# The second layer's gate and value products: four of six token groups in pairs by Strassen's seven block products

## The chip, the cores and the metric

The kernel runs on one core of a Trainium2 chip. The metric is the device time of one execution in microseconds; the median of three runs is quoted. In the profile PE is the matrix engine (TensorE) and PEld its weight loads, DVE is VectorE, ACT is ScalarE, POOL is GpSimd, and SP is the engine whose queue issues the DMAs. PE reads operands from SBUF and writes to PSUM, which has eight banks of 512 fp32 columns by 128 partitions. "2.4 GHz" is the clock that the profile shows as a granted clock of 1.00.

## What is computed

Attention with a block-causal mask over 4 x 8 heads of 576 positions and 64 dimensions gives 2304 tokens of 512 features. Two feed-forward layers follow; the change lies in the second.

```python
x = attention(q, k, v)                  # (2304, 512), tokens by features
h = x @ w_in                            # 512 -> 2048
x = (h - tanh(h)) @ w_out               # 2048 -> 512
xn = x / sqrt(mean(x * x) + 1e-6) * rms_g
g = xn @ w_gate                         # 512 -> 1536
val = xn @ w_val                        # 512 -> 1536
out = (silu(g) * val) @ w_out2          # 1536 -> 512
```

The weights arrive as float64 and are turned into fp32 on the chip, from pairs of 32-bit words.

## The kernel before

Tokens are taken in six groups of 384 (`NG`, `TG`), each three tiles of 128 (`TT`). The hidden features of the second layer go in twelve units of 128 (`J2`). To keep fp32 accuracy, every operand of a product is held as a high part (rounded to fp32r) and a low part (the rest); a product is three matmuls, high by high, high by low and low by high. ACT rounds the high part (`rnd`, L98) and DVE subtracts it for the low part (`lo`, L103).

Second layer, from L849: for each group `n` and unit `j`, PE makes the gate product and the value product. Each takes four slices of 128 input features by three matmuls of 384 columns (L862 to L864), twelve in all, into a PSUM bank of the pool `gvp` (four banks). ACT applies SiLU to the gate (L871), DVE multiplies by the value (L872), ACT and DVE split the result into `gh`, `gl`. The output matmuls of the unit before follow (`out2`, `gemm_out` L679 to L681: nine of 512 columns, into one PSUM accumulator for each token tile). After unit 11 the accumulators are copied out (L843, L845) and stored.

The inputs of the next group are prepared in units 3 to 8: `xn_a` loads a tile and scales it (L710), `xn_b` transposes it on PE (four transposes of 128x128, L718) and splits it.

The second layer's weights stay in SBUF, as high and low parts. There are 36 pieces of [128, 512] (`w2_piece`): gate, value and output weights of each unit. Each is loaded (`stage`), made into floats (`convert`: two passes on ACT, L133 and L135, three on DVE, L136 to L138) and split. 18 pieces are made during the first layer's last group, 18 during the second layer's first group.

What sets the order: PE's instructions run as the code is written (`manual_schedule`), those of the other engines in an order that a scheduler fixes when the program is built; each engine executes its queue strictly in order. SP's queue carries all the DMAs named here.

Of the kernel before, what the change touches and what calls it, by code (L numbers as in the profile page):

```python
# [49 lines left out]
EARLY = 7  # L50

# [38 lines left out]
def build(ctx, tc, q, k, v, w_in, w_out, w_gate, w_val, w_out2, rms_g, ident_in, out):  # L90
# [18 lines left out]
    w1f = [drm.tile([128, 1024], F32, name=f"w1f_{j}") for j in range(J1 // 2)]  # L109
    w1d = [[drm.tile([128, 1024], F32, name=f"w1d_{x}_{j}") for j in range(J1)] for x in "io"]  # L110
# [461 lines left out]
    with tc.manual_schedule(engines={PE.engine}):  # L572
# [133 lines left out]
        def xn_a(n, t):  # L706
            c = n * TT + t
            x = w2a.tile([128, DM], F32, name="xin", tag="xin", bufs=2)
# [15 lines left out]
        w2 = {}  # L724

        def w2_piece(n, pool):
            j, part = divmod(n, 3)
            if part == 0:
                w2[j] = [[pool.tile([128, 512], F32R, name=f"w2_{j}_{x}_{y}") for y in "hl"] for x in range(3)]
            st = stage(rows_(w_out2, j) if part == 2 else cols((w_gate, w_val)[part], j))  # L730
            convert(st, *w2[j][part])
# [4 lines left out]
        npc = 0  # L736
        nld = J1
        for s in range(NSA):
# [54 lines left out]
            if j == J1 - 1:  # L793
                while att.pos < goal:
                    att.step()
                if g == NG - 2:
# [4 lines left out]
                    env["stg"] = sw.enter_context(tc.tile_pool(name="st2", bufs=3, side="right"))  # L801
# [4 lines left out]
            if g == NG - 1:  # L806
# [6 lines left out]
                for _ in range(2 if j % 7 == 3 else 1):  # L813
                    w2_piece(npc, w2a)
                    npc += 1
# [9 lines left out]
        gvp = ctx.enter_context(tc.tile_pool(name="gvp", bufs=2, space=PSUM))  # L825
# [3 lines left out]
        def out2(s, t):  # L829
            n, j = divmod(s, J2)  # L830
            if j == 0:
                accs[t] = accp.tile([128, DM], F32, name=f"acc{t}", tag=f"acc{t}")
            gh, gl = gts[s]
            wh, wl = w2[j][2]
            gemm_out(accs[t], gh, gl, wh, wl, t, j == 0, j == J2 - 1)
            if j == J2 - 1:
                c = n * TT + t
                if s == NSB - 1 and t == TT - 1:
                    o = w2a.tile([128, DM], F32, name="xin", tag="xin", bufs=2)
                else:  # L840
                    o = wk.tile([128, DM], F32, name="x2s", tag="x2s")
# [7 lines left out]
        NSB = NG * J2  # L849
        for s in range(NSB):  # L850
            n, j = divmod(s, J2)
            if n == 0 and npc < 3 * J2:
                w2_piece(npc, w2b)
                npc += 1
            xh, xl = xt("B", n)
            gv = []
            for part in range(2):
                ps = gvp.tile([128, TG], F32, name=f"gv{part}", tag=f"gv{part}")
# [7 lines left out]
                if part == 0:  # L866
                    if n == 0 and npc < 3 * J2:
                        w2_piece(npc, w2b)
                        npc += 1
# [17 lines left out]
        for t in range(TT):  # L887
            out2(NSB - 1, t)
# [20 lines left out]
```

## Time and profile before

| | |
|---|---|
| median of three runs | 1095.95 us (1094.66 to 1096.4) |
| span of the profiled execution | 1093.2 us |
| PE busy | 1067.0 us (98%), 5696 matmuls |
| DVE busy | 613.8 us (56%) |
| ACT busy | 542.6 us (50%) |
| POOL busy | 158.5 us (14%), none of it after about 560 us |
| DMA | 172.3 MB |

The profiled execution's own device time is not given apart from its span. Matmuls overlap in the record, so PE's busy share says only that it was rarely empty; what a matmul takes is seen from the starts of neighbours. The second layer's first product starts at 626.6 us, so that layer takes the last 467 us of the span.

### The profile page before, as it was taken

How to read it: one execution, taken by the hardware profiler on the slowest of the kernel's cores; microseconds unless marked ns; L12 is line 12 of the kernel's file. 1: busy time of each engine (PE TensorE's matmuls, PEld its weight loads, DVE VectorE, ACT ScalarE, POOL GpSimd, SP SyncE). 2: the span in 40 equal slices, each digit the busy share in tenths (PEclk: the TensorE clock that was granted, in tenths of full speed). 3: DMA queues.
4: the chain of work that ended last, by engine and by line, in shares of the span. 5: the costliest groups of instructions: out<-in, count | busy, mean ns of one | idle time of the engine just before them, and what ended most of it. 6: DMA issues, size and time to landing. Idle time of an engine off the chain costs nothing.

```text
span 1093.2 us, 16380 instructions
## 1 busy us (share of the span) xinstructions
PE 1067.0 (98%) x5696; PEld 951.3 (87%) x5696; DVE 613.8 (56%) x1403; ACT 542.6 (50%) x1271; POOL 158.5 (14%) x276
## 2 busy tenths in 40 slices
PE   7799989999999999999999999999999999999998
PEld 5576669998889999999999899899999999999997
DVE  5888857777678766676567889622222222222212
ACT  5777757667677665566556687512112111111111
POOL 5531201123323232323300000000000000000000
PEclk8999999999999999999999999999999999999999
DMA  9788888988777979766589855200000000000000
GB/s 217 230 282 296 264 285 261 285 218 232 178 188 201 249 212 240 224 203 192 157 299 395 294 165 183 83 34 21 29 10 20 29 11 20 29 11 1 29 1 30
DMA packets 166962, 172.32 MB, mean 158 GB/s; under 512 B 108000, under 2 KB 131680, under 8 KB 166880
## 3 DMA queue, kind: packets, MB, share of 16 engines
q1 hardware_dynamic: 166880, 171.28, 52.0%
q8 instruction: 45, 0.74, 0.3%
q14 instruction: 37, 0.30, 0.1%
HBM read 140.84 MB, written 30.41 MB: 157 GB/s over the span
## 4 chain that ended last, share of the span: by engine, by line
PE 91%; ACT 3%; DVE 3%; DMA 1%; issue 1%; SPq 0%; POOL 0%; DVEq 0%
PE acc L681 9%; PE acc L679 9%; PE acc L680 9%; PE gv L864 9%; PE gv L862 9%; PE gv L863 9%; PE t L766 6%; PE t L768 6%; PE t L767 6%; PE t L462 5%; PE t L503 3%; PE acc L689 3%; PE t L527 2%; PE t L556 2%; PE t L536 1%
## 5 line engine op out<-in xcount | busy, mean ns | idle before, releaser
L862 PE MATMUL gv<-xh,w_h 128*128 128x384 f32 x576 | 195.3, 339 | 0.0
L864 PE MATMUL gv<-xh,w_l 128*128 128x384 f32 x576 | 194.0, 337 | 0.7 <-DVE w_l L103 0.7
L863 PE MATMUL gv<-xl,w_h 128*128 128x384 f32 x576 | 193.8, 337 | 0.0
L872 DVE TENSOR_TENSOR gt<-gv,gt 128x384 f32<-128x384 f32 x72 | 40.1, 557 | 238.9 <-PE gv L864 237.2
L98 ACT ACTIVATE gh<-gt 128x384 fp32r<-128x384 f32 x152 | 79.4, 522 | 167.3 <-DVE gt L872 136.6
L766 PE MATMUL t<-xh,w 128*128 128x384 f32 x384 | 137.7, 359 | 0.0
L768 PE MATMUL t<-xh,w 128*128 128x384 f32 x384 | 129.8, 338 | 0.0
L767 PE MATMUL t<-xl,w 128*128 128x384 f32 x384 | 129.5, 337 | 0.0
L871 ACT ACTIVATE gt<-gv 128x384 f32<-128x384 f32 x72 | 35.2, 489 | 161.9 <-PE gv L864 161.9
L103 DVE TENSOR_TENSOR gl<-gt,gh 128x384 fp32r<-128x384 f32 x152 | 89.1, 586 | 39.0 <-ACT gh L98 38.7
L862 PEld LDWEIGHTS gv<-xh,w_h 128*128 128x128 f32 x576 | 108.3, 188 | 2.8 <-ACT w_h L98 0.3
L863 PEld LDWEIGHTS gv<-xl,w_h 128*128 128x128 f32 x576 | 108.3, 188 | 2.5
L864 PEld LDWEIGHTS gv<-xh,w_l 128*128 128x128 f32 x576 | 108.2, 188 | 1.0 <-DVE w_l L103 1.0
L477 ACT ACTIVATE pt<-pt,stat 128x64 f32<-128x64 f32 (+2 forms) x144 | 80.3, 559 | 45.8 <-DVE pt L475 44.6
L679 PE MATMUL acc<-w,gh 128*128 128x512 f32 x240 | 98.2, 409 | 0.0
L681 PE MATMUL acc<-w,gl 128*128 128x512 f32 x240 | 94.9, 395 | 0.0
L680 PE MATMUL acc<-w,gh 128*128 128x512 f32 x240 | 94.4, 393 | 0.0
L681 PE MATMUL acc<-w_h,gl 128*128 128x512 f32 x216 | 85.6, 396 | 0.1
L680 PE MATMUL acc<-w_l,gh 128*128 128x512 f32 x216 | 85.3, 395 | 0.0
L679 PE MATMUL acc<-w_h,gh 128*128 128x512 f32 x216 | 84.8, 393 | 0.5 <-ACT gh L98 0.5
L766 PEld LDWEIGHTS t<-xh,w 128*128 128x128 f32 x384 | 72.3, 188 | 3.6 <-issue 0.7
L767 PEld LDWEIGHTS t<-xl,w 128*128 128x128 f32 x384 | 72.5, 189 | 2.2
(114 smaller groups left out, 2014.4 us busy)
## 6 DMA issues: line engine op xcount, KB each, us to landing
w<-w1d_i SPq DMA_DIRECT2D x80, 512.0 KB, 4.7
w<-w1d_o SPq DMA_DIRECT2D x64, 512.0 KB, 4.5
st<-in_moe_w_out SPq DMA_DIRECT2D x28, 512.0 KB, 4.1
st<-in_moe_w_in SPq DMA_DIRECT2D x16, 512.0 KB, 5.0
w1d_i<-w SPq DMA_DIRECT2D x16, 512.0 KB, 4.3
w1d_o<-w SPq DMA_DIRECT2D x16, 512.0 KB, 3.6
st<-in_moe_w_gate SPq DMA_DIRECT2D x12, 512.0 KB, 4.1
st<-in_moe_w_val SPq DMA_DIRECT2D x12, 512.0 KB, 3.8
```

The source lines that it names most:

```text
L98: ACT.activation(out=o, in_=i, func=AF.Copy)
L103: eng.tensor_tensor(out=o, in0=full, in1=hi.bitcast(F32), op=ALU.subtract)
L477: ACT.activation(out=pt[:, 0:keys], in_=pt[:, 0:keys], func=AF.Exp, scale=-1.0, bias=least, accum_out=st[:, 8 + ti:9 + ti])
L679: PE.matmul(acc, lhsT=gh[:, c], rhs=wh, start=first, stop=False)
L680: PE.matmul(acc, lhsT=gh[:, c], rhs=wl, start=False, stop=False)
L681: PE.matmul(acc, lhsT=gl[:, c], rhs=wh, start=False, stop=last)
L766: PE.matmul(h, lhsT=wh[:, c], rhs=xh[:, kk], start=(kk == 0), stop=False)
L767: PE.matmul(h, lhsT=wh[:, c], rhs=xl[:, kk], start=False, stop=False)
L768: PE.matmul(h, lhsT=wl[:, c], rhs=xh[:, kk], start=False, stop=(kk == KD - 1))
L862: PE.matmul(ps, lhsT=wh[:, c], rhs=xh[:, kk], start=(kk == 0), stop=False)
L863: PE.matmul(ps, lhsT=wh[:, c], rhs=xl[:, kk], start=False, stop=False)
L864: PE.matmul(ps, lhsT=wl[:, c], rhs=xh[:, kk], start=False, stop=(kk == KD - 1))
```

## The change

Groups 1 and 2 still run plainly, but together, unit by unit, as the first pair. Groups 3 and 4, and 5 and 6, run as pairs by Strassen's scheme (in its form with seven products and shared sums): the gate and value weights of a unit, cut into two halves of 256 input features each, are a 2 x 2 block matrix, and the two groups' inputs in the same halves are another. The four blocks of the result (gate and value of either group) come from seven block products (`fast`), each of two slices by three matmuls, six matmuls of 384 columns. In exchange:

- four sums of weight blocks for each unit (`unit_sums`: POOL makes the sums, ACT and DVE split them), and the units' own parts, are stored to HBM (`w2d`) in the first pair, and read back for each unit of each later pair (`load_unit`, two units ahead, three buffers);
- four sums of input blocks for each token tile (`pair_a`, on POOL) and 14 transposes in place of twice four (`pair_b`);
- seven additions in the place where products were only read: DVE adds products to `c11`, `c12`, `c21`, `c22`, ACT copies the first;
- SiLU and the value product of the second group of a pair are kept in SBUF (`later`), and its output matmuls run after the pair's twelve units, unit after unit; between them stand the transposes for the next pair.

All twelve units' weights are now made as full floats first (`unit_piece`), kept for four units at a time; 8 of these pieces and 6 of the output weights are made in the first layer's last group, the rest during the first pair.

```diff
+        def unit_piece(j, part):
+            if part == 0:
+                full[j] = w0.tile([128, 2, 512], F32, name="fu", tag="fu", bufs=4)
+            f = full[j]
+            convert(stage(cols((w_gate, w_val)[part], j)), f[:, part])
+            if part == 1:
+                w2[j] = w = w0.tile([128, 2, 2, 512], F32R, name="wu", tag="wu", bufs=4)
+                rnd(ACT, w[:, 0], f)
+                lo(DVE, w[:, 1], f, w[:, 0])
+
+        def unit_sums(j):
+            f = full.pop(j).rearrange("p g (k c) -> p (g k) c", k=2)
+            g_l, g_u, v_l, v_u = (f[:, n] for n in range(4))
+            o = w0.tile([128, 4, 256], F32, name="fs", tag="fs")
+            POOL.tensor_tensor(out=o[:, 0], in0=v_u, in1=v_l, op=ALU.add)
...
+            w = w0.tile([128, 2, 4, 256], F32R, name="ws", tag="ws")
+            pin(ACT.activation(out=w[:, 0], in_=o, func=AF.Copy))
+            lo(DVE, w[:, 1], o, w[:, 0])
+            pin(SP.dma_start(out=w2d[0][j], in_=w2[j].rearrange("p x g c -> p x (g c)")[:, :, 0:768].bitcast(F32)))
+            SP.dma_start(out=w2d[1][j], in_=w.rearrange("p x g c -> p x (g c)").bitcast(F32))
...
-        gvp = ctx.enter_context(tc.tile_pool(name="gvp", bufs=2, space=PSUM))
+        gvp = ctx.enter_context(tc.tile_pool(name="gvp", bufs=4, space=PSUM))
...
+        def plain(j, n):
+            w = w2[j].rearrange("p x g c -> p g x c")
+            xh, xl = xt("B", n)
+            for part in range(2):
+                ps = bank()[:, 0:TG]
+                product(ps, w[:, part, 0], w[:, part, 1], xh, xl)
+                if part == 0:
+                    gt = wk.tile([128, TG], F32, name="gt", tag="gt")
+                    ACT.activation(out=gt, in_=ps, func=AF.Silu)
+                else:
+                    DVE.tensor_tensor(later[j] if n else gt, ps, gt, ALU.mult)
+                    if n == 0:
+                        gts[j] = split(gt)
...
+                if part == 0:
+                    if n == 0:
+                        unit_sums(j)
+                    if j + 4 < J2:
+                        unit_piece(j + 4, n)
...
+            ACT.activation(out=c11, in_=prod(wa, 1, xa, 1), func=AF.Copy)
+            DVE.tensor_tensor(c21, prod(wb, 1, xc, 0), c11, ALU.add)
+            DVE.tensor_tensor(c12, prod(wb, 0, xb, 1), c21, ALU.add)
+            ps = prod(wb, 2, xc, 1)
+            DVE.tensor_tensor(c22, ps, c12, ALU.add)
+            DVE.tensor_tensor(c21, ps, c21, ALU.add)
+            DVE.tensor_tensor(c11, prod(wa, 0, xa, 0), c11, ALU.add)
+            ACT.activation(out=gt, in_=c11, func=AF.Silu)
+            DVE.tensor_tensor(c12, prod(wb, 3, xb, 0), c12, ALU.add)
+            ACT.activation(out=c12, in_=c12, func=AF.Silu)
+            POOL.tensor_tensor(out=later[j], in0=c12, in1=c22, op=ALU.mult)
+            DVE.tensor_tensor(c21, prod(wa, 2, xd, 0), c21, ALU.add)
+            DVE.tensor_tensor(gt, c21, gt, ALU.mult)
+            gts[j] = split(gt)
...
+            for j in range(J2):
+                g = split(later[j])
                 for t in range(TT):
-                    out2(s - 1, t)
-                gts.pop(s - 1)
...
+                    out2(2 * p + 1, j, t, g)
+                if p + 1 < NG // 2:
+                    if j in (1, 3, 8):
+                        pair_b((1, 3, 8).index(j), x)
+                    if j in (2, 6):
+                        (pair_load if j == 2 else pair_a)(p + 1, 2)
```

How the order moves on the engines, at three places. First DVE while the weights are prepared, in the second layer's first group before (`cv` and `cu` are the pieces in conversion, `w_7_0_l` the low part of a finished piece, `gt` and `gl` a unit's product and its low part, `xl` the next input):

```order
L137 SCALAR_TENSOR_TENSOR cv<-cv,cu 128x512 x2
L138 SCALAR_TENSOR_TENSOR cv<-st,cv 128x512 x2
L872 TENSOR_TENSOR gt<-gv_7928,gt 128x384
L103 TENSOR_TENSOR w_7_0_l<-cv,w_7_0_h 128x512
L103 TENSOR_TENSOR w_7_1_l<-cv,w_7_1_h 128x512
L103 TENSOR_TENSOR gl<-gt,gh 128x384
L136 TENSOR_SCALAR cv<-cv 128x512
```

And in the first pair now, around units 5 and 6 (`fu` is a unit as full floats, `wu` its split, `ws` the split of its sums `fs`, `gs_7587` the second group's kept product):

```order
L105 TENSOR_TENSOR gl<-gt,gh 128x384
L140 SCALAR_TENSOR_TENSOR cv<-cv,cu 128x512
L105 TENSOR_TENSOR wo_l<-cv,wo_h 128x512
L141 SCALAR_TENSOR_TENSOR fu<-st,cv 128x512
L911 TENSOR_TENSOR gs_7587<-gv,gt 128x384
L139 TENSOR_SCALAR cv<-cv 128x512
L140 SCALAR_TENSOR_TENSOR cv<-cv,cu 128x512
L141 SCALAR_TENSOR_TENSOR fu<-st,cv 128x512
L105 TENSOR_TENSOR ws<-fs,ws 128x1024
L911 TENSOR_TENSOR gt<-gv,gt 128x384
L105 TENSOR_TENSOR wu<-fu,wu 128x1024
```

The two low parts of 1024 columns stand among the products that free PSUM, and the one of `ws` waits for POOL and ACT.

Second PE where one group's accumulators end and the next one's begin, before (`w2_10_2_h` is unit 10's output weights, `gv0_10570` the next group's first gate product):

```order
L679 MATMUL acc2_10114<-w2_10_2_h_8035,gh_10515 128x512
L680 MATMUL acc2_10114<-w2_10_2_l_8036,gh_10515 128x512
L681 MATMUL acc2_10114<-w2_10_2_h_8035,gl_10516 128x512
L862 MATMUL gv0_10570<-xh_10247,w2_0_0_h_6814 128x384
L863 MATMUL gv0_10570<-xl_10248,w2_0_0_h_6814 128x384
```

And now, at the end of the first pair's units (`acc0_8898` is the second group's first accumulator):

```order
L684 MATMUL acc0_7723<-wo_11_h_8587,gl_8814 128x512
L682 MATMUL acc1_7727<-wo_11_h_8587,gh_8813 128x512
L683 MATMUL acc1_7727<-wo_11_l_8588,gh_8813 128x512
L684 MATMUL acc1_7727<-wo_11_h_8587,gl_8814 128x512
L682 MATMUL acc2_7731<-wo_11_h_8587,gh_8813 128x512
L683 MATMUL acc2_7731<-wo_11_l_8588,gh_8813 128x512
L684 MATMUL acc2_7731<-wo_11_h_8587,gl_8814 128x512
L682 MATMUL acc0_8898<-wo_0_h_7020,gh_8894 128x512
```

The new group's output matmuls follow at once, with six matmuls instead of a unit's products between the last use of an accumulator and its next.

Third DVE where the last token tile of the next inputs is scaled, before (`xin_8748` the tile, `xl_8604` the low part of the inputs after the transposes):

```order
L872 TENSOR_TENSOR gt_8719<-gv1_8721,gt_8719 128x384
L103 TENSOR_TENSOR gl_8736<-gt_8719,gh_8735 128x384
L710 SCALAR_TENSOR_TENSOR xin_8748<-xin_8748,rinv_106,g_bc_6761 128x512
L872 TENSOR_TENSOR gt_8764<-gv1_8766,gt_8764 128x384
L103 TENSOR_TENSOR gl_8781<-gt_8764,gh_8780 128x384
L103 TENSOR_TENSOR xl_8604<-t_8793,xh_8603 128x4x128
```

And now, in the run of output matmuls between two pairs (`xn_8962` holds the tiles of both groups):

```order
L105 TENSOR_TENSOR gl_9031<-gs6_7588,gh_9030 128x384
L105 TENSOR_TENSOR gl_9050<-gs7_7589,gh_9049 128x384
L105 TENSOR_TENSOR gl_9063<-gs8_7590,gh_9062 128x384
L978 SCALAR_TENSOR_TENSOR xn_8962<-xn_8962,rinv_130,g_bc_6788 128x512
L978 SCALAR_TENSOR_TENSOR xn_8962<-xn_8962,rinv_130,g_bc_6788 128x2x256
L105 TENSOR_TENSOR gl_9102<-gs9_7591,gh_9101 128x384
```

The scaling of this tile comes behind the split of unit 8; POOL's differences and PE's 14 transposes follow it.

## Rows read from the trace of the kernel before

**Rows 1.** Stretches: us, busy us of each engine, PE's granted clock, DMA share, GB/s

```profile
200.00:500.00 300.00, 295.85 (x1671) 270.61 (x1670) 219.25 (x562) 197.12 (x496) 88.14 (x134) 1.00 0.79 218
600.00:620.00 20.00, 20.00 (x105) 17.88 (x104) 16.38 (x29) 12.66 (x24) 0.00 (x0) 1.00 0.90 336
660.00:680.00 20.00, 20.00 (x110) 18.74 (x109) 18.09 (x34) 13.35 (x27) 0.00 (x0) 1.00 0.54 169
750.00:800.00 50.00, 50.00 (x266) 46.78 (x265) 11.62 (x21) 9.33 (x18) 0.00 (x0) 1.00 0.07 26
```

**Rows 2.** Page, chain that ended last, shares by engine

```profile
PE 91%; ACT 3%; DVE 3%; DMA 1%; issue 1%; SPq 0%; POOL 0%; DVEq 0%
```

**Rows 3.** PE's waits, 590 us to the end: waited for, us, times, longest

```profile
PE gv L864 <- DVE w_l L103: 0.7, 1, 0.7
PE acc L679 <- ACT gh L98: 0.5, 1, 0.5
```

**Rows 4.** Timeline of PE in group 3: start us, us, instruction

```profile
799.79 0.34 PE L862 MATMUL gv<-xh,w_h 128*128 128x384 f32 x1
...
803.49 0.40 PE L679 MATMUL acc<-w_h,gh 128*128 128x512 f32 x1
...
805.58 0.34 PE L862 MATMUL gv<-xh,w_h 128*128 128x384 f32 x1
```

**Rows 5.** Timeline around four transposes

```profile
735.09 0.60 PE L718 MATMUL t<-ident,xin 128*128 128x128 f32 x4
...
735.70 0.33 PE L863 MATMUL gv<-xl,w_h 128*128 128x384 f32 x1
```

**Rows 6.** Groups by line, 700 to 1050 us: count, busy us, mean ns, idle before

```profile
L862 PE MATMUL gv<-xh,w_h 128*128 128x384 f32 x438 | 148.5, 339 | 0.0
...
L681 PE MATMUL acc<-w_h,gl 128*128 128x512 f32 x165 | 65.3, 396 | 0.0
...
L103 DVE TENSOR_TENSOR gl<-gt,gh 128x384 fp32r<-128x384 f32 x55 | 30.7, 558 | 29.0 <-ACT gh L98 29.0
L872 DVE TENSOR_TENSOR gt<-gv,gt 128x384 f32<-128x384 f32 x55 | 30.7, 557 | 208.0 <-PE gv L864 208.0
L98 ACT ACTIVATE gh<-gt 128x384 fp32r<-128x384 f32 x55 | 28.9, 525 | 119.6 <-DVE gt L872 119.6
...
L710 DVE SCALAR_TENSOR_TENSOR xin<-xin,rinv,g_bc 128x512 f32<-128x512 f32 x12 | 9.0, 746 | 0.0
...
L718 PE MATMUL t<-ident,xin 128*128 128x128 f32 x48 | 7.2, 272 | 0.0
...
L845 DVE COPY x2s<-acc 128x512 f32<-128x512 f32 x10 | 6.9, 691 | 9.0 <-DMA out<-x2s 8.6
```

**Rows 7.** Groups by line, 595 to 700 us, where weights are converted

```profile
L137 DVE SCALAR_TENSOR_TENSOR cv<-cv,cu 128x512 int32<-128x512 int32 x29 | 19.9, 689 | 2.2
...
L138 DVE SCALAR_TENSOR_TENSOR cv<-st,cv 128x512 int32<-128x512 int32 x28 | 19.1, 684 | 0.1
L103 DVE TENSOR_TENSOR w_l<-cv,w_h 128x512 fp32r<-128x512 f32 x28 | 19.1, 687 | 2.6 <-ACT w_h L98 2.4
...
L136 DVE TENSOR_SCALAR cv<-cv 128x512 f32<-128x512 f32 x29 | 12.2, 421 | 0.0
```

**Rows 8.** Groups of POOL, 100 to 560 us

```profile
L103 POOL TENSOR_TENSOR xl<-xs,xh 128x192 fp32r<-128x192 f32 x16 | 10.1, 630 | 9.1 <-ACT xh L98 9.1
...
L103 POOL TENSOR_TENSOR xl<-xs,xh 128x384 fp32r<-128x384 f32 x8 | 8.3, 1037 | 1.0 <-ACT xh L98 0.9
```

**Rows 9.** Groups of DVE, 200 to 500 us, where POOL is at work

```profile
L103 DVE TENSOR_TENSOR gl<-gt,gh 128x384 fp32r<-128x384 f32 x48 | 30.2, 630 | 4.4 <-ACT gh L98 4.2
L780 DVE TENSOR_TENSOR gt<-t,gt 128x384 f32<-128x384 f32 x48 | 26.4, 550 | 21.0 <-ACT gt L774 20.9
```

**Rows 10.** Page, DMA packets of the whole span

```profile
DMA packets 166962, 172.32 MB, mean 158 GB/s; under 512 B 108000, under 2 KB 131680, under 8 KB 166880
```

**Rows 11.** DMA issues by line, 540 to 700 us: count, KB each, us to landing

```profile
w<-w1d_o SPq DMA_DIRECT2D x16, 512.0 KB, 8.0
```

More of the change, by code (lines that the diff above doesn't have):

```diff
@@ L109, in build @@
     w1f = [drm.tile([128, 1024], F32, name=f"w1f_{j}") for j in range(J1 // 2)]
+    w2d = [[drm.tile([128, 2, n], F32, name=f"w2d_{n}_{j}") for j in range(J2)] for n in (768, 1024)]
     w1d = [[drm.tile([128, 1024], F32, name=f"w1d_{x}_{j}") for j in range(J1)] for x in "io"]
@@ L707, in xn_a @@
             c = n * TT + t
-            x = w2a.tile([128, DM], F32, name="xin", tag="xin", bufs=2)
+            x = w2a.tile([128, DM], F32, name="xin", tag="xin", bufs=4)
             SP.dma_start(out=x, in_=x2d[c * 128:(c + 1) * 128, :])
@@ L812, in build @@
                     xn_b(0, (j - 10) // 2)
-                for _ in range(2 if j % 7 == 3 else 1):
-                    w2_piece(npc, w2a)
-                    npc += 1
+                if j > 12:
+                    xn_a(1, j - 13)
+                if pieces:
+                    pieces.pop(0)()
         for t in range(TT):
@@ new lines, in plain, with load_unit @@
+                if n == 0 and 2 * j + part in (0, 1, 3):
+                    xn_b(1, (0, 1, 3).index(2 * j + part))
+                if part == 0:
[3 more added lines that the diff above has]
+                        unit_piece(j + 4, n)
+            if n and j in LATEOUT:
+                out_piece(EARLYOUT + LATEOUT.index(j))
+        def load_unit(s):
+            j = s % J2
+            if s < NG // 2 * J2:
+                ws[s] = (tp.tile([128, 2, 768], F32R, name="wa", tag="wa", bufs=3),
+                         tp.tile([128, 2, 1024], F32R, name="wb", tag="wb", bufs=3))
+                for o, d in zip(ws[s], w2d):
+                    SP.dma_start(out=o.bitcast(F32), in_=d[j])
@@ new lines, in build, with pair_load, pair_a @@
+        xn = {}
+        def pair_load(p, t):
+            x = xn[t] = w2b.tile([128, 8, 256], F32, name="xn", tag="xn", bufs=2)
+            c1, c2 = 2 * p * TT + t, (2 * p + 1) * TT + t
+            SP.dma_start(out=x[:, 0:2], in_=x2d[c1 * 128:(c1 + 1) * 128, :].rearrange("p (k c) -> p k c", k=2))
+            SP.dma_start(out=x[:, 2:8:5], in_=x2d[c2 * 128:(c2 + 1) * 128, :].rearrange("p (k c) -> p k c", k=2))
+        def pair_a(p, t):
+            x = xn[t]
+            c1, c2 = 2 * p * TT + t, (2 * p + 1) * TT + t
+            g2 = g_bc.rearrange("p (k c) -> p k c", k=2)
+            for xv, c in ((x[:, 0:2], c1), (x[:, 2:8:5], c2)):
+                pin(DVE.scalar_tensor_tensor(xv, xv, rinv[:, c:c + 1], g2, ALU.mult, ALU.mult))
+            for o, m, n in ((3, 7, 1), (5, 2, 7), (4, 2, 3), (6, 0, 4)):
+                POOL.tensor_tensor(out=x[:, o], in0=x[:, m], in1=x[:, n], op=ALU.subtract)
@@ new lines, in pair_b @@
+        def pair_b(t, x):
+            src = xn.pop(t)
+            for n, (xh, xl) in enumerate(x):
+                nk = xh.shape[1]
+                ps = bank()
+                for kk in range(nk):
+                    PE.transpose(ps[:, kk * 128:(kk + 1) * 128],
+                                 src[:, 2 * n + kk // 2, kk % 2 * 128:kk % 2 * 128 + 128], ident)
+                tv = ps[:, 0:nk * 128].rearrange("p (k c) -> p k c", k=nk)
+                hv, lv = (y[:, :, t * 128:(t + 1) * 128] for y in (xh, xl))
+                rnd(ACT, hv, tv)
+                lo(DVE, lv, tv, hv)
```

131 lines of the change are left out of this document (83 added, 48 removed).

## The prediction

> **What bounds the kernel now.** I read the stretches first: in the second layer TensorE (PE) is busy in every microsecond, at the granted clock 1.00 (2.4 GHz), while VectorE (DVE) and ScalarE (ACT) fall from 90% and 67% in a stretch that still converts weights to 23% and 19% later, and the 16 DMA engines from 0.9 to 0.07 [rows 1]. The chain that ended last says the same, 91% PE [rows 2]. PE's own waits from 590 us to the end add up to 1.2 us [rows 3]. So in this layer a matmul that is taken out shortens the span by its pitch, as long as the rest keeps up. A busy figure is no pitch here, because matmuls overlap; I take pitches from starts. From 799.79 to 803.49 lie 21 matmuls of 384 columns: 0.176 us each; from 803.49 to 805.58 nine of 512: 0.232 [rows 4]. Four transposes hold the next products up from 735.09 to the second product at 735.70, 0.61 us, less one product of 0.176: 0.43, or 0.11 each [rows 5]. Check over 350 us: 3 x 438 x 0.176 + 3 x 165 x 0.232 + 48 x 0.11 = 351 us [rows 6]; the pitches carry the whole stretch.
>
> **Matmuls removed.** A unit (128 gate and 128 value columns) of two groups takes 2 x 2 x 12 = 48 matmuls of 384 columns before and 7 x 6 = 42 after. Six fewer, 12 units, two pairs of groups: 144 x 0.176 = 25.3 us. The 648 output matmuls stay.
>
> **Transposes added.** The pairs transpose 14 blocks per tile of 128 tokens (four for each of three combined inputs, two for the fourth) instead of eight: 6 x 3 x 2 = 36 more. 36 x 0.11 = 4.0 us, all on PE. Net 21.3 us.
>
> **Preparation, the first pair.** This is the part that can give time back. Groups 1 and 2 still run plainly, but now all twelve units are also converted to full floats, split, combined into four sums on GpSimd (POOL), split again and stored to HBM. Take units 0 to 7, in which units 4 to 11 are converted. PE there: 16 halves x 24 x 0.176 + 8 x 9 x 0.232 = 84.3 us. DVE: 16 conversions of 0.421 + 0.689 + 0.684 = 1.79, 28.7 us; 16 low parts of 1024 columns, no such row, between one and two rows of 512 (0.687 to 1.37), taken at 1.37 since the 384 and 512 rows grow with the columns, 21.9; five output pieces of 1.79 + 0.69, 12.4; 16 gate-times-value products of 0.557, 8.9; eight splits of 0.558, 4.5; three for group 2's inputs at 0.69 like other 512-column splits, 2.1 [rows 6, 7]. Sum 78.5 us, 93% of PE's 84.3. POOL's 32 sums of 256 columns have no row; 192 columns take 0.63 and 384 take 1.04 [rows 8], so between those, 0.77, 3.1 us per unit, 24.6 in all, on an engine that was idle here.
>
> Do they disturb DVE? While POOL was 29% busy (88.1 of 300 us), a DVE split, both inputs in SBUF, took 0.630 us; with POOL silent it takes 0.558; a DVE operation that reads PSUM and SBUF took 0.550 and is 0.557 without POOL [rows 1, 6, 9]. So only DVE instructions with two SBUF inputs pay, 13% at that share. POOL's share here would be 3.1 of 10.5 us, about the same; 67.5 of the 78.5 us have two SBUF inputs (or run over SBUF alone): plus 8.8, 87.3 us against 84.3, DVE 3 us behind at the end of unit 7. The other bound is that each POOL sum stops DVE fully: 24.6 us less at most the 11 that read PSUM, so 13.6 to 24.6 more, 8 to 19 us behind. Before PE feels it: four PSUM banks, each wanted again after three other products of 2.11 us, so 6.3 us of slack. PE would lose 0 by the first bound, 2 to 13 by the second. I take 3 us, nearer to the row, since the row was measured under the same POOL share. The Trainium skill, "SBUF — State Buffer", section "SBUF: two separate sides", states the second bound as a rule: VectorE and GpSimd share one port pair, as an exclusive lock for the whole instruction, also where a VectorE instruction has two SBUF inputs and GpSimd reads SBUF. The rows agree with who pays; that each overlap costs a whole instruction they do not settle, so it is a rival below.
>
> The rest of this part lies beside PE. ACT's two 1024-column roundings per unit are new, on an engine at 67% in such a stretch before, while its conversions spread over twice the time [rows 1]. Stores: 1.84 MB per unit (768 and 1024 columns, high and low, 128 rows) and 1.3 MB of loads in 10.5 us, about 300 GB/s; the kernel ran 336 at a DMA share of 0.90 [rows 1]. Behind each store of sums on SP's queue stand the next weight loads, and ACT's next rounding of sums waits for that store to land; 512 KB loads took 8.0 us to land under the heaviest load [rows 11], so 1 MB takes between that, if latency rules, and 16, if bytes do, against 10.5 per unit. At 16 ACT would fall behind; the buffers are four units deep, so I put nothing here and leave it to the range.
>
> **Pair units.** Per unit PE needs 42 x 0.176 + 9 x 0.232 = 9.48 us, DVE nine operations of 0.557, 5.0 us. A product now ends every 1.06 us, and four banks leave 3.2 us to read one; the most that DVE does between is two adds, 1.1 us. Nothing charged. The weights of a unit, 1.84 MB, must come every 9.48 us, 194 GB/s, two units ahead; nothing charged.
>
> **Second group of a pair, alone.** Output matmuls now run 108 in a row, 25.1 us with only splits beside them: 0.525 us on ACT and 0.558 on DVE against 2.09 on PE [rows 6]; covered. Two new tight places. First, the accumulators turn over with no products between: a copy of 0.691 [rows 6] has 1.39 us of other accumulators' matmuls to hide behind; 0 to 0.56 each if one more DVE operation is ahead of it, three times; I take 0. Second, the third token tile: in DVE's order its scaling stands behind the split of unit 8, which needs the buffer that unit 6's matmuls release at 17.7 us of this stretch. Then 0.52 + 0.56 + 2 x 0.746 [rows 6] and POOL's four differences, 3.1: 23.4 us or, with the handovers between, 24; PE reaches the last of the transposes at 23.2. About 0.7 us, twice: 1.4 (0 to 4, if the differences run at the 384-column row).
>
> **Sum.** 1093.2 - 25.3 + 4.0 + 3 + 1.4 = 1076.3 us of span. Before, the median is 1095.95 against a profiled span of 1093.2, 2.75 more; so 1079 us, 1.5% less. The 1.2 us of old waits I leave in. A difference of 0.2%, 2.2 us, is about what a measurement of this kernel can tell from no change.
>
> **Rivals.** (a) *POOL and DVE exclude each other* in the preparation: another 5 to 10 us there, 1084 to 1091; 1087 as its middle. For it: 93% on DVE before any disturbance. Against: at about 90% DVE before, PE waited 1.2 us in all [rows 1, 3]. (b) *The add chain sets the pair units*: adds depend on each other and on ACT's first copy, in DVE's strict order. If one add of 0.56 per unit reached PE: 24 x 0.56 = 13 us, 1092; two, 1106. Against: 5.0 of 9.48 us on DVE, and after almost every unit 2.09 us of output matmuls let it catch up. (c) *Slower than before: the weight stream.* Three units lie ready when a pair starts; the other nine must come in the ten units' time between, 94.8 us. At r GB/s a unit takes 1835/r us. To eat the 17 us and 2 more, each pair must lose 9.5 us: 104.3 us for nine units, 11.6 each, r = 158. Below 158 GB/s, which is the mean of the whole span [rows 10], the change is slower; at 140 it loses 23 us a pair, 1125. Against it: 336 GB/s between 600 and 620 us [rows 1], and these transfers are in long rows.
>
> **Chances.** Forecast (1073 to 1084) 0.72; (a) 0.17; (b) 0.06; (c) 0.05. Range: low end all new waits zero and the old 1.2 gone, 1093.2 - 21.3 - 1.2 + 2.75 = 1073; high end 1090, most of (a); outside lie (b), (c) and the far end of (a). Faster by over 0.2%: 0.72 + 0.17 and half of (b), less a little: 0.90; within 0.2%: half of (b) and a little, 0.05; slower 0.05.
>
> **What would show it.** Three lines of products with 528 matmuls instead of 576 each, at the same 0.176 pitch; the time from the first product of the second layer to the end some 17 us shorter. PE's waits in the first 85 us of the layer: under 6 us for the forecast, 8 or more for (a), with the DVE splits there well over 0.63 us. For (b), PE waits on DVE adds in every pair unit; for (c), PE waits on the loaded weights. What I hold weakest is the 3 us of the preparation, whose order of work no row of before shows.

## The result and the profile after

The changed kernel takes 1081.93 us (1080.89 to 1084.42, four runs) against 1096.18 for the kernel before, measured beside it (four runs): a ratio of 0.9873, 95% interval 0.9856 to 0.9890. It is faster, by 14 us; 1079.0 was forecast, 2.9 less, and 1081.93 lies well inside 1073 to 1090. The profiled execution has a span of 1079.1 us and a device time of 1080.89; before, the span was 1093.2.

To compare profiles I cut the span at matmuls that both kernels have. All numbers are worked out from starts in the timeline.

| stretch, us | before | after |
|---|---|---|
| start to the last 144 output matmuls of the first layer | 562.38 | 562.80 |
| from there to the second layer's first product (the last group) | 64.18 | 66.75 |
| second layer's first product to the first pair unit (T2) | | 162.22 |
| first pair unit to the end (T3) | | 287.34 |
| second layer, T2 + T3 | 466.65 | 449.56 |

So the second layer gave 17.1 us, where the prediction's terms add up to 16.9, and the last group of the first layer took 2.6 back, for which the prediction had no term. The first 560 us, whose code is the same in every kernel here, end between 561.2 and 566.3 us in the profiles below; that scatter is why stretches, not spans, are compared. A stretch whose code is unchanged repeats within 0.4 us, but for one wait in the first pair, which made T2 of e7 0.6 us longer.

Stretches after, as in [rows 1] (us, busy us of PE, weight loads, DVE, ACT and POOL, granted clock, DMA share, GB/s): the preparation in two parts, and the pair units.

```profile
629.00:714.00 85.00, 82.00 (x449) 78.35 (x448) 75.49 (x102) 54.28 (x90) 30.17 (x28) 1.00 0.81 286
714.00:760.00 46.00, 45.48 (x246) 43.53 (x246) 34.53 (x45) 20.29 (x34) 23.39 (x24) 1.00 0.61 225
...
800.00:900.00 100.00, 100.00 (x544) 96.14 (x543) 60.15 (x101) 21.96 (x43) 16.41 (x19) 1.00 0.54 201
```

PE has no gap in the pair units; it has some in the preparation, where DVE is busy for 89% of the first 85 us. The chain that ended last, as in [rows 2], went from 91% PE to:

```profile
PE 82%; DVE 7%; DMA 4%; ACT 4%; issue 2%; SPq 0%; POOL 0%; DVEq 0%; POOLq 0%; ACTq 0%
```

PE's waits from 560 us to the end, as in [rows 3] (us, times, longest). The first layer's are the two on `gl` (1.1) and 0.3 of those on `gh`; the other 0.4 on `gh` stand at the ends of the two pairs' units. A wait here is shorter than the time lost by starts (0.2 against 0.64 us at each of these ends), because matmuls overlap in the record.

```profile
PE t L721 <- DVE xl L105: 2.2, 1, 2.2
PE acc L684 <- DVE gl L105: 1.1, 2, 0.6
PE gv L873 <- DVE xl L105: 0.8, 1, 0.8
PE acc L682 <- ACT gh L100: 0.7, 3, 0.3
PE gv L872 <- ACT gt L909: 0.5, 1, 0.5
PE gv L988 <- POOL xn L980: 0.3, 1, 0.3
```

PE in the second pair, as in [rows 4] (start, us, instruction): where a unit's output matmuls begin, and the next unit's products.

```profile
968.84 0.39 PE L682 MATMUL acc<-wo_h,gh 128*128 128x512 f32 x1
...
970.93 0.34 PE L872 MATMUL gv<-xh,wa 128*128 128x384 f32 x1
```

The unit before had its output matmuls at 959.39 and its first product at 961.48: 7.36 us for 42 products and 2.09 for nine output matmuls, 9.45 in all, and the ten units of each pair that stand between the output matmuls of others repeat it within 0.03 us. Where two of the three rivals put their loss, nothing happens.

DMA moves more, as in [rows 10]:

```profile
DMA packets 179639, 238.43 MB, mean 221 GB/s; under 512 B 109152, under 2 KB 134368, under 8 KB 174944
```

DVE in the first 85 us of the second layer, groups as in [rows 7] (count, busy us, mean ns, idle before), and POOL's sums in the first pair, for which [rows 8] gave only other sizes:

```profile
L139 DVE TENSOR_SCALAR cv<-cv 128x512 f32<-128x512 f32 x18 | 12.9, 720 | 0.3
...
L105 DVE TENSOR_TENSOR gl<-gt,gh 128x384 fp32r<-128x384 f32 x7 | 6.6, 938 | 0.0
...
L911 DVE TENSOR_TENSOR gt<-gv,gt 128x384 f32<-128x384 f32 x7 | 3.9, 551 | 0.0
```

```profile
L751 POOL TENSOR_TENSOR fs<-fu 128x256 f32<-128x256 f32 x11 | 13.1, 1193 | 124.0 <-DVE ws L105 124.0
L752 POOL TENSOR_TENSOR fs<-fu 128x256 f32<-128x256 f32 x11 | 12.0, 1092 | 0.0
```

A split of 384 columns takes 0.938 us here, against 0.558 in [rows 6] with POOL silent and 0.630 in [rows 9]; the scaling pass L139, which reads one tile of SBUF and writes it back, takes 0.720 against 0.421 in [rows 7]; a product that reads PSUM takes 0.551, as ever. Eleven of the twelve units' sums are in this count: those of unit 0 ran at 569 us, in the first layer's last group.

### The profile page after: what moved, and what is told of

Read it like the earlier page. It is cut to its first block, busy times and chain, and to the rows that moved or that the text cites. A ratio compares the mean times of both kernels' runs of the same rounds, so it can differ in the third digit from the quotient of the medians.

```text
span 1079.1 us, 16811 instructions
## 1 busy us (share of the span) xinstructions
PE 1049.6 (97%) x5588; PEld 932.4 (86%) x5588; DVE 741.7 (69%) x1559; ACT 568.2 (53%) x1307; POOL 253.3 (23%) x372
## 4 chain that ended last, share of the span: by engine, by line
PE 82%; DVE 7%; DMA 4%; ACT 4%; issue 2%; SPq 0%; POOL 0%; DVEq 0%; POOLq 0%; ACTq 0%
PE acc L682 8%; PE acc L684 8%; PE acc L683 8%; PE gv L873 8%; PE gv L872 7%; PE gv L874 7%; PE t L799 5%; PE t L801 5%; PE t L800 5%; PE t L465 5%; PE t L506 3%; PE acc L692 3%; PE t L530 2%; PE t L559 2%; DMA w<-w1d_i 2%
## 5 line engine op out<-in xcount | busy, mean ns | idle before, releaser
L682 PE MATMUL acc<-wo_h,gh 128*128 128x512 f32 x216 | 85.7, 397 | 0.4 <-ACT gh L100 0.4
L684 PE MATMUL acc<-wo_h,gl 128*128 128x512 f32 x216 | 85.3, 395 | 0.0
L683 PE MATMUL acc<-wo_l,gh 128*128 128x512 f32 x216 | 84.9, 393 | 0.0
L799 PEld LDWEIGHTS t<-xh,w 128*128 128x128 f32 x384 | 72.4, 189 | 3.6 <-issue 0.7
L100 ACT ACTIVATE pp<-t 128x512 fp32r<-128x512 f32 (+6 forms) x152 | 64.2, 437 | 21.1 <-PE t L506 20.4
L478 DVE TENSOR_SCALAR_CACHE_REDUCE pt<-t 128x64 f32<-128x64 f32 (+2 forms) x144 | 64.0, 449 | 16.2 <-PE t L465 15.0
L801 PEld LDWEIGHTS t<-xh,w 128*128 128x128 f32 x384 | 72.1, 188 | 0.0
L959 POOL TENSOR_TENSOR gs<-c,c 128x384 f32<-128x384 f32 x24 | 24.4, 1015 | 201.4 <-ACT c L958 201.4
L813 DVE TENSOR_TENSOR gt<-t,gt 128x384 f32<-128x384 f32 x80 | 44.2, 553 | 39.5 <-ACT gt L807 39.3
L506 PE MATMUL t<-ident,pt 128*128 128x128 f32 x400 | 65.8, 274 | 3.7 <-POOL pt L493 2.4
L807 ACT ACTIVATE gt<-t 128x384 f32<-128x384 f32 x96 | 46.6, 485 | 40.4 <-PE t L801 40.0
```

What stands on the lines that cost most here:

```text
L100: ACT.activation(out=o, in_=i, func=AF.Copy)
L506: PE.transpose(t[:, (j - a) * 128:(j - a + 1) * 128], pt[:, j * 128:(j + 1) * 128], ident)
L682: PE.matmul(acc, lhsT=gh[:, c], rhs=wh, start=first, stop=False)
L683: PE.matmul(acc, lhsT=gh[:, c], rhs=wl, start=False, stop=False)
L684: PE.matmul(acc, lhsT=gl[:, c], rhs=wh, start=False, stop=last)
L799: PE.matmul(h, lhsT=wh[:, c], rhs=xh[:, kk], start=(kk == 0), stop=False)
```

## The experiments

The stretches are those of the table above; T2 holds the preparation and the second group's output matmuls, T3 everything from the first pair unit on. Where a stretch is not given it agrees with the changed kernel within 0.4 us.

### The price of a product (e1)

```diff
-            DVE.tensor_tensor(c21, prod(wa, 2, xd, 0), c21, ALU.add)
+            ps = prod(wa, 2, xd, 0)
+            c = slice(512, 768)
+            product(ps, wa[:, 0, c], wa[:, 1, c], xd[0][:, 0:2], xd[1][:, 0:2])
+            DVE.tensor_tensor(c21, ps, c21, ALU.add)
```

> The seventh product of every pair unit is run twice into the same bank, so that a pair unit has 48 matmuls again, as two plain groups have; the adds, the sums and the weight stream stay. Theory (TensorE alone sets the pair units, so a product is worth its matmuls): 24 x 6 x 0.175 = 25.2 us more than the changed kernel's 1081.9, 1107. Rival (part of a unit's time is set by the add chain or the stream, so that PE has slack): less than 20 us more, below 1102.

Measured: 1105.82 us, ratio 1.0084 [1.0067, 1.0101] to the kernel before: with an eighth product in place of the one saved, the change is slower than before. T3 311.47 instead of 287.34, so 24.1 us for 144 matmuls. At the two ends of the pairs' units e1 takes 8.54 us for 36 output matmuls where the changed kernel takes 8.96; with these 0.8 us the matmuls cost 25.0, 0.173 each. The saved product is what the change lives on, at full price.

### POOL's sums and DVE (e2)

The four sums are left out, and the weights themselves are split in their place.

```diff
-            o = w0.tile([128, 4, 256], F32, name="fs", tag="fs")
-            POOL.tensor_tensor(out=o[:, 0], in0=v_u, in1=v_l, op=ALU.add)
...
+            o = f
```

> Leaves out POOL's four weight sums per unit in the first pair (the unit's own blocks are split and stored in their place, so the pairs' results are not the reference's); ACT, DVE and DMA work stays. Theory A (POOL slows DVE but the slack of four banks takes most of it): DVE's split of a unit's product falls from 0.94 to about 0.56 us, its scaling pass from 0.72 to 0.42, and PE's waits in the preparation fall by 1 to 2 us, 1080 to 1081. Theory B (the exclusion of POOL and DVE is the main cause of what PE loses in the preparation): PE's waits there fall by 4 us or more, 1078 or less. If POOL does not disturb DVE, the durations stay.

Measured: 1079.70 us (1078.93 to 1080.30), T2 161.02, 1.2 less. The same groups of DVE, with POOL silent:

```profile
L139 DVE TENSOR_SCALAR cv<-cv 128x512 f32<-128x512 f32 x20 | 8.3, 420 | 0.8 <-ACT cv L136 0.5
...
L105 DVE TENSOR_TENSOR gl<-gt,gh 128x384 fp32r<-128x384 f32 x8 | 4.4, 550 | 0.0
```

and its stretches:

```profile
629.00:714.00 85.00, 82.81 (x453) 79.29 (x452) 68.78 (x112) 59.11 (x97) 0.00 (x0) 1.00 0.91 315
714.00:760.00 46.00, 46.00 (x249) 44.08 (x249) 23.69 (x36) 16.70 (x29) 5.73 (x8) 1.00 0.46 176
```

POOL's sums cost DVE 75.49 + 34.53 - 68.78 - 23.69 = 17.6 us over the whole preparation. The prediction's bounds, 8.8 and 13.6 to 24.6, were made for units 0 to 7, the first 85 us; there the groups' means give some 14 (L139 alone 18 x 0.30), the low end of the second bound. But PE feels little of them. The waits of 0.8 on `xl` and 0.5 on `gt` are gone, and the first pair's units take 128.2 us instead of 130.0; 0.6 us is lost again at the third token tile, which leaves the 1.2 of T2. The longest wait, 2.2 before the transposes, stays: that one is not POOL's doing. Nor are the other two POOL's alone, since they are gone in e4 as well, where POOL makes all its sums.

### The transposes' bank and the square root (e3, e5)

e3 gives the transposes no bank of their own but a fifth in the products' pool. e5 moves the square root for the last three token tiles from the start of the second layer to unit 8, so that ACT need not change its table there.

```diff
-        rms(15, 18)
         sps.close()
...
+            if n and j == 8:
+                rms(15, 18)
             if n and j in LATEOUT:
```

> Group 2's three input tiles are transposed into the products' pool, which gets five banks, in place of a bank of their own. Theory (PE's wait of 2.4 us before the second of these transposes is for that single bank, which ACT's two table loads keep from being read): the wait goes, 1079.5. Rival (ACT and DVE are late anyway, the wait only moves to the next product or to the inputs themselves): at most 1 us less, 1081 to 1082.

> The square root for the last three token tiles, with ACT's two table loads of 1.28 us around it, moves from the start of the second layer to unit 8 of the first pair; nothing else changes. Theory (these loads hold ACT up so that group 2's inputs are rounded late; PE's waits of 2.2 and 0.8 us there are theirs): both waits shrink to under 0.5 in sum and the time falls by about 2 us, to 1080. Rival (DVE, busy with conversions left over from the first layer, is what is late): PE still waits 2 us or more there, 1082.

Measured: e3 1081.24 us, T2 162.21, unchanged to 0.01 us. The wait before the transposes is gone and others have come:

```profile
PE acc L684 <- DVE gl L105: 3.1, 4, 1.7
PE gv L873 <- DVE xl L105: 1.3, 1, 1.3
```

So the bank was only the place where PE noticed; what ACT and DVE had to do was late, and PE then waited for the split of a unit's product and for the inputs. e5: 1079.45 us (1077.86 to 1084.19), T2 160.43, 1.8 less, and its wait before the transposes is

```profile
PE t L721 <- DVE xl L105: 0.6, 1, 0.6
```

What was late is seen on ACT in the changed kernel (start, us, instruction, idle before):

```profile
631.91 1.28 ACT L909 ACT_TABLE_LOAD   x1 [0.18 <-PE gv L874]
633.20 0.49 ACT L909 ACTIVATE gt<-gv 128x384 f32<-128x384 f32 x1
633.71 1.28 ACT L704 ACT_TABLE_LOAD   x1
635.01 0.30 ACT L704 ACTIVATE rinv<-ssq,epsq 128x3 f32<-128x3 f32 x1
635.21 0.58 ACT L100 ACTIVATE xh<-t 128x512 fp32r<-128x512 f32 x1
635.69 1.04 ACT L756 ACTIVATE ws<-fs 128x1024 fp32r<-128x1024 f32 x1
635.82 0.69 DVE L105 TENSOR_TENSOR xl<-t,xh 128x512 fp32r<-128x512 f32 x1 [0.31 <-ACT xh L100]
```

The first transposes of group 2's inputs start at 631.66; their rounding waits behind two table loads, SiLU's and the square root's, 2.56 us, and the next transposes wait for it until 636.57. With the square root elsewhere 1.6 of the 2.4 us lost there are gone. SiLU's load stays in e5.

### The first layer's last group (e4, e6)

e4 takes two of the six output pieces out of the last group and makes them in units 9 and 10 of the first pair. e6 is e4 and e5 together, and the square root of the first 15 tiles moved from unit 5 of the last group to unit 1.

```diff
-EARLYOUT = 6
-LATEOUT = (1, 2, 4, 5, 7, 8)
+EARLYOUT = 4
+LATEOUT = (1, 2, 4, 5, 7, 8, 9, 10)
```

> Two of the six output-weight pieces that are made during the first layer's last group are made in the first pair instead, as its last two. Theory (the first layer's last group loses its 2.3 us because conversions stand ahead of its splits, which have little slack): that group gets 1 to 2 us back, and the first pair, with DVE 75% busy in its last third, takes the pieces for nothing: 1080 to 1081. Rival (DVE in the preparation has no room left): the first pair loses as much or more, 1082 or above.

> The late square root of the run beside it, the first square root moved from unit 5 to unit 1 of the first layer's last group, and two output-weight pieces made in the first pair instead of that group. Theory: what PE loses around the change of layers (2.3 us in the last group, 3 at the start of the second layer) mostly goes, 1077 to 1078, the fastest of these. Rival (the lost time is DVE's total work there, so it reappears later in the preparation): 1080 or above.

Measured: e4 1079.00 us (1077.15 to 1080.80), but the last group takes 67.96 us, 1.2 more than in the changed kernel; T2 is 159.79, 2.4 less, since the first pair's waits of 0.8 and 0.5 us are gone and its longest is 0.4 shorter. e6 1079.92 us (1077.32 to 1082.48), last group 68.37, T2 158.59. Its two largest waits from 560 us on:

```profile
PE acc L682 <- ACT gh L100: 2.6, 4, 1.9
PE acc L684 <- DVE gl L105: 0.6, 1, 0.6
```

Less work in the last group did not shorten it. In the changed kernel it loses 1.4 of its 2.6 us at the last 18 output matmuls, which take 5.58 instead of 4.21:

```profile
624.88 0.55 DVE L813 TENSOR_TENSOR gt<-t,gt 128x384 f32<-128x384 f32 x1
624.99 1.06 ACT L100 ACTIVATE wu<-fu 128x1024 fp32r<-128x1024 f32 x1 [0.27 <-DVE fu L141]
625.96 0.51 ACT L100 ACTIVATE gh<-gt 128x384 fp32r<-128x384 f32 x1
626.08 1.23 DVE L105 TENSOR_TENSOR wu<-fu,wu 128x1024 fp32r<-128x1024 f32 x1 [0.66 <-ACT wu L100]
...
627.23 0.55 DVE L105 TENSOR_TENSOR gl<-gt,gh 128x384 fp32r<-128x384 f32 x1
```

The product `gt` is ready at 625.43; its rounding stands behind 1.06 us for `wu` on ACT, its low part behind 1.23 us for `wu` on DVE. With 512 columns a piece, before, a low part in the way took 0.69 [rows 7]. In e4, e6 and e12 these 18 matmuls still take 5.6 us; in e12 the same two `wu` instructions stand ahead. Another 0.9 us go at 588 us, where no 1024-column instruction stands ahead of the late split: the load of the table for tanh starts 1.1 us after the square root, behind two conversion passes of ACT, where before it followed at once, and two passes of DVE come before the split. POOL's sums of unit 0 are not it: without them, in e2, the group takes 67.03. The loss hangs on which instruction stands ahead of which, and moving pieces re-deals that; the version that doesn't lose there was not found.

### The end of a pair's units (e7)

The product kept for the second group is made by DVE, after the unit's own split, and not by POOL.

```diff
-            POOL.tensor_tensor(out=later[j], in0=c12, in1=c22, op=ALU.mult)
...
             gts[j] = split(gt)
+            DVE.tensor_tensor(later[j], c12, c22, ALU.mult)
```

> The product of the second group of a pair is taken from POOL to DVE, behind DVE's other work of the unit; one more DVE operation per pair unit. Theory (POOL holds up DVE's product of the first group, 0.97 us for 0.56, and this is what makes PE wait 0.6 us at each of the two ends of a pair's units): DVE's product falls to 0.56, PE's waits there to under 0.2, the pair units stay at 9.45 us although DVE does ten operations: 1 us less, 1081. Rival (DVE's chain of adds is near its limit): pair units grow above 9.45 us, 2 us or more in all.

Measured: 1081.98 us (1079.02 to 1084.34). T3 is 287.07, 0.27 less: at the end of each pair's units 36 output matmuls take 8.82 us instead of 8.96, where 8.32 would be free of loss. A median can't show that, nor T3 by itself: e4 and e6, which leave the pairs alone, have 287.07 and 287.08. T2 is 162.81, 0.6 more, by a longer wait in the first pair. What happens at the end of a pair's units, in the changed kernel:

```profile
901.40 1.01 POOL L959 TENSOR_TENSOR gs<-c,c 128x384 f32<-128x384 f32 x1 [2.44 <-ACT c L958]
901.85 0.97 DVE L961 TENSOR_TENSOR gt<-c,gt 128x384 f32<-128x384 f32 x1
902.86 0.52 ACT L100 ACTIVATE gh<-gt 128x384 fp32r<-128x384 f32 x1 [1.54 <-DVE gt L961]
```

POOL's product runs to 902.41; DVE's, begun at 901.85, ends at 902.82, 0.41 us after POOL, where it takes 0.56 alone. Both read two SBUF operands. PE's next output matmul, the first of unit 11, is due at 903.06 and starts at 903.44: between that unit's last product and its output matmuls stand only the nine of unit 10. The accumulators are not what it waits for; the first matmul into the next group's accumulator, at 905.75, follows its neighbour by the usual 0.23. In e1, where an extra product keeps the two apart, POOL is done before DVE begins, and only 0.22 of the 0.64 us are lost:

```profile
911.38 1.01 POOL L959 TENSOR_TENSOR gs<-c,c 128x384 f32<-128x384 f32 x1 [2.87 <-ACT c L958]
912.87 0.56 DVE L964 TENSOR_TENSOR gt<-c,gt 128x384 f32<-128x384 f32 x1
```

In e7 POOL is out of the way, but DVE's kept product runs from 901.96, ahead of the unit's own, which then starts at 902.43: the order set by the scheduler, not by the code, put it there, and most of what was won went into that.

### The weight stream (e8, e9, e10)

e8 copies each block once more, HBM to HBM, where it is read. e10, whose edit is shown, writes each block, once read into SBUF, back to a spare place in HBM; e9 does so with the 1024-column blocks alone. Each ran once.

```diff
                 for o, d in zip(ws[s], w2d):
                     SP.dma_start(out=o.bitcast(F32), in_=d[j])
+                for n in (0, 1):
+                    SP.dma_start(out=spare[n][j], in_=ws[s][n].bitcast(F32))
```

> With each unit's weights the same 1.84 MB are also copied within HBM, so that the DMA engines carry about twice the stream's traffic during the pairs. Theory (the stream has room: DMA share 0.52 at 193 GB/s): the share in the pair units rises towards 1 and a unit's weights land later, but two units ahead is enough; PE's waits in pair units stay under 5 us in all, 1082 to 1087. Rival (the stream is close to the edge): PE waits for weights in most units, 1095 or more.

> Each unit's 1024-column block, once read into SBUF in a pair, is also written back to a spare place in HBM: 1.05 MB more per unit, and the buffer is free only once that store is done. Unlike the copies of e8, these stores cannot run before the pairs, since they need the tile that was just read. 2.88 MB per 9.45 us unit is 305 GB/s, below the 371 to 381 that the copies of e8 moved. Theory (the stream has room, the prediction's bound of 158 GB/s is far): 22 full units of a pair still take 7.36 and 2.08 us, no wait on wa or wb above 0.3 us, time within 2 us of 1081.9. Rival (SP's queue, which now stands still at each store until the load has landed, sets the stream): waits of PE on wb or wa, 0.5 us a unit or more, 1090 or more.

> Both blocks of each unit are written back: 3.67 MB per unit, 388 GB/s at the pace of PE, more than the 381 that the copies of e8 reached. Theory (a rate sets the stream, and three units lie ready): in each pair 9 units to read and 11 to write back, 36.7 MB, take 96 to 105 us at 381 to 350 GB/s, against 94.5 us of PE: a loss of 2 to 10 us a pair, by waits of PE on wa or wb in the pairs' later units, 1085 to 1102. If SP's standing still at each store counts more than the rate, more than 10 us a pair, above 1102. If nothing is lost, the stream of the changed kernel has at least twice the room it needs.

Measured: e8 1148.29 us, but not in the place that it was meant to load. A copy from HBM needs nothing but the stored block, so in SP's queue they stood right behind the stores: 47 of the 48, for both pairs, were issued before the first pair unit. T2 227.42, T3 286.96. In the first pair the DMA engines then run at their full share:

```profile
660.00:700.00 40.00, 40.00 (x217) 38.40 (x216) 29.73 (x44) 20.51 (x33) 6.67 (x9) 1.00 0.98 371
```

and PE waits for inputs and weights that come late:

```profile
PE gv L991 <- DVE xl L105: 26.2, 2, 25.1
PE gv L873 <- ACT wu L100: 21.8, 3, 8.3
```

It says nothing of the pairs' stream, only that the preparation has no room for that much more DMA. e9 1088.40 us, e10 1091.69. In e10 the first pair's units run at

```profile
800.00:900.00 100.00, 100.00 (x544) 96.11 (x543) 59.92 (x101) 22.38 (x44) 14.07 (x15) 1.00 0.94 357
```

357 GB/s at a DMA share of 0.94, and every unit still takes 7.36 and 2.09 us: no wait on weights anywhere. What e9 and e10 lose lies elsewhere: T2 grows by 5.2 (e9) and 5.0 us (e10), T3 by -0.4 and 5.9. It is the run of the second group's output matmuls, at the transposes of the third token tile. PE's waits in e10's first such run:

```profile
PE gv L991 <- DVE xn L981: 1.8, 1, 1.8
PE gv L991 <- POOL xn L983: 1.3, 2, 0.9
```

In that run the tile's load, behind two of the stores in SP's queue, is issued at 771.75 instead of 767.53 and lands at 785.02 instead of 779.58. But DVE, whose order is fixed when the program is built, now has the tile's scaling behind the split of unit 10, where the changed kernel had it behind that of unit 8, and it goes from the one to the other without a gap; the order alone gives the delay. In e10's second run the tile has landed at 923.16, and still DVE comes to it only behind unit 10's split (unit 6's in the changed kernel):

```profile
933.49 1.41 DVE L981 SCALAR_TENSOR_TENSOR xn<-xn,rinv,g_bc 128x512 f32<-128x512 f32 x2
```

e9's second run, where the scaling stands where the changed kernel has it, loses nothing. Part of the loss in the other runs is a lower clock (last section).

So my rate theory was wrong: 388 GB/s asked, 357 moved, and PE never waited for weights. That the rival's in-order queue costs anything is not shown either: a load was issued 4.2 us late, but DVE's order hides what that is worth.

### Two banks instead of four (e11)

```diff
-        gvp = ctx.enter_context(tc.tile_pool(name="gvp", bufs=4, space=PSUM))
+        gvp = ctx.enter_context(tc.tile_pool(name="gvp", bufs=2, space=PSUM))
```

> The pool of the second layer's products has two PSUM banks in place of four. The prediction put the pair units at nothing because four banks leave 3.2 us to read a product; with two banks 1.06 us are left. Theory (the chain of adds is short, but not shorter than one product): the product that is read twice takes 2 x 0.557 and a handover, over 1.06 us, so a wait of 0.2 to 1 us in each of the 24 pair units, 5 to 24 us; in the first pair the slack falls from 6.3 to 2.1 us, and PE loses 3 to 10 us more there: 1090 to 1115. Rival (b) (the chain sets the pair units once it is close to the edge): every one of seven products waits, 3 us a unit or more, above 1150. If the pair units stay at 9.45 us, the four banks were never needed there.

Measured, in one run: 1107.20 us. A pair unit takes 7.70 + 2.09 us, 0.34 more; the first pair's units 136.0 us instead of 130.0; and each of the six batches of 14 transposes takes 2.87 us instead of 1.45, which I had not in the sum. 24 x 0.34 + 6.0 + 6 x 1.42 - 0.7 (the third batch was late in the changed kernel anyway) = 22.0, against 22.9 in T2 + T3. The 0.34 are taken where the product read by two adds returns its bank (from 827.70 to 828.09, 0.21 us more than a pitch of 0.18) and in smaller steps. In the first pair:

```profile
PE gv L872 <- DVE gs L911: 3.4, 6, 0.9
```

Six units in which DVE is behind by up to 0.9 us beyond the slack of one bank. Four banks hide this in the changed kernel, where the same six units take 8.45 us for their 48 products, against 9.1 to 10.0 here.

### Three edits together (e12)

e4, e5 and e7 in one kernel.

> Three of the earlier edits at once: the square root for the last three tiles at unit 8 (e5), two output pieces moved to the first pair (e4), the kept product on DVE (e7). If they add up: PE waits on transposes fall from 2.2 to under 0.8 us, the waits of the last group of the first layer by 0.5, the turnovers from 1.2 to 0.6: span 2.5 to 3 us shorter than 1079.1, median 1078.5 to 1079.5. If each only moved its wait to the next place, 1080.5 to 1082.

Measured, five runs: 1078.04 us (1075.65 to 1079.83), ratio 0.9842 [0.9828, 0.9855], against 0.9873 [0.9856, 0.9890] for the changed kernel: 0.3% faster than it, by intervals that just don't touch, each taken against its own runs of the kernel before. T2 158.63, 3.6 less; T3 286.78, 0.6 less, half of it at the ends of the pairs' units; the last group 66.84, no gain. All waits from 560 us on:

```profile
PE acc L684 <- DVE gl L105: 1.1, 2, 0.6
PE t L721 <- DVE xl L105: 0.6, 1, 0.6
PE gv L989 <- POOL xn L981: 0.3, 1, 0.3
PE acc L682 <- ACT gh L100: 0.3, 1, 0.3
```

## Why the prediction was right, and where it was not

The direction, the mechanism of the gain and its size held. Term by term for the second layer, measured from starts:

| term, us | predicted | measured |
|---|---|---|
| 144 matmuls fewer | -25.3 | -25.3, and 0.7 more: pair products at 0.1753, not 0.176 |
| 36 transposes more | +4.0 | +3.7 (14 in 1.45) |
| preparation | +3, and 1.2 of old waits left in | +4.4, and the old 1.2 gone |
| accumulators' turnover | 0 | 0 |
| last unit's split at the end of a pair's units | no term | +1.3 (36 output matmuls in 8.96 instead of 8.32, twice) |
| third token tile | +1.4 | +0.7, once |
| pair units, stream | 0 | 0 |
| sum | -16.9 | -17.1 |

That the sums agree within 0.2 us is luck in part: errors of up to 1.4 us in single terms cancel.

**The missing term: the last group of the first layer.** The step that failed is "ACT's two 1024-column roundings per unit are new [...] while its conversions spread over twice the time", which looked at the second layer alone. The same new instructions stand in the first layer's last group, where unit 0 to 3's weights are made, and the group takes 2.6 us more: 1.4 of them behind the rounding and the low part of `wu`, 0.9 where conversion passes stand ahead of a table load and a split. Which instructions stand ahead is shown; that taking work out cures it is not: e4, e6 and e12 had 67.96, 68.37 and 66.84.

**Preparation: right in size, wrong in cause.** I took 3 us for POOL slowing DVE, by a 13% that a row showed at about the same POOL share (29%, here 35%). In the trace a DVE split was slowed by 68%, and POOL's sums took 1.08 us each, not 0.77. e2 shows that all of the slowing is POOL's: the cost to DVE is 17.6 us, some 14 of them in the first 85 us, the low end of the second bound. The Trainium skill, "SBUF — State Buffer", section "SBUF: two separate sides", had it so: one engine holds the shared port pair for a whole instruction and the other stands still. The trace agrees nearly to the full: DVE ended 0.41 us after POOL, where by the rule it would be 0.56. What saved the forecast is the other half of rival (a): I let DVE be behind "at the end of unit 7" of work that I had put into 84 us, but the order lets it run on to unit 11, 110.0 us of DVE work in 131 us, and four banks take the rest; two banks don't (e11). So without POOL's sums PE wins 1.8 us in the first pair, 1.2 in T2 (e2); rival (a) had 8 or more. Of its two signs one came, splits well over 0.63 us (0.938); the other did not, since PE lost 3.7 us in the first 85, under the forecast's 6. As e4 wins the same 1.8 by moving two output pieces, POOL's slowing and DVE's other work had to come together. The larger part, 2.4 us, stands behind ACT's two table loads ahead of one rounding, which the prediction did not list; e5 removes 1.6 of it.

**Turnover: right, but the loss stands beside it.** "0 to 0.56 each [...] I take 0": the accumulators turn over without a loss. Nine matmuls earlier, two of the three ends lose 0.64 us for which the prediction had no term: the last unit's split has nine output matmuls to hide behind, not the next unit's products. About 0.42 of it is POOL's product, which holds DVE's up and does not in e1; e7, with one more DVE operation in POOL's place, wins 0.14.

**Pair units and stream: as predicted, and with room.** Rival (b) falls: no wait in any unit, DVE 60% busy; it would take two banks to lose 0.34 us a unit. Rival (c), deciding at 158 GB/s, falls too: 201 GB/s flow without a wait, and 357 in e10. That the change does what it says is e1.

**From span to median.** I added 2.75 us to the span; in the profiled run it is 1.8. The span missed by 2.8 (1079.1 against 1076.3), and the median lies 1.0 above the profiled run, so the total misses by 2.9.

## What to carry to other kernels

Count new instructions in every stage that the order lets them into, also the one before the stage that is changed: a long instruction ahead of a short one on which TensorE waits can cost up to its own length. Bound a slowed engine against the whole time in which its work may be done and against the buffers between it and TensorE, since 17.6 us lost on VectorE cost TensorE 1.8 at most. Compare kernels by stretches between matmuls that they share; medians with a scatter of 3 us hide what such stretches mostly repeat within 0.4. An edit can move the order of engines that it doesn't touch, so look where a late instruction stands before blaming what it reads.

## What the runs showed of the hardware

A wait of TensorE can cost more than its length. In e9 the third batch of transposes waited for its tile three times, 1.29, 0.37 and 0.92 us, with only transposes between. The granted clock then went to 0.50, the lower of the two levels (1.2 GHz), from 789 to 796 us; the 27 output matmuls behind the batch took 8.40 us instead of 6.24:

```profile
786.00:791.00 5.00, 2.42 (x14) 1.60 (x14) 2.51 (x4) 1.72 (x3) 2.81 (x4) 0.81 0.89 359
791.00:793.00 2.00, 2.00 (x7) 1.71 (x7) 1.02 (x2) 0.87 (x2) 0.00 (x0) 0.50 0.10 28
793.00:796.00 3.00, 3.00 (x8) 2.32 (x8) 0.38 (x1) 0.52 (x1) 0.00 (x0) 0.51 0.56 162
796.00:800.00 4.00, 4.00 (x19) 3.33 (x19) 1.00 (x3) 0.60 (x1) 0.00 (x0) 1.00 0.00 0
```

In e10 it fell at both third batches (788 to 792 and 935 to 942 us). The waits of up to 2.2 us in the changed kernel had no such effect (granted clock 1.00 from 629 to 900 us). At about 292 to 301 us, in code that no kernel here touches, the clock fell to 0.50 for some 3 us in the profiles of the changed kernel and of e1, e4, e5, e6, e8, e9 and e11, and not in those of e2, e3, e7, e10 and e12 nor before; in e6, e8 and e11 also at 146 to 154 us. What decides it was not found.
